# Softmax row sums of an attention block: ones-matmuls on TensorE, or accumulating DMAs through DRAM

## The chip, the cores and the metric

The kernel runs on one core of a Trainium2 chip. The metric is the device time of one execution in microseconds (us); lower is better. The engines are TensorE (PE, and PEld for its weight loads), VectorE (DVE), ScalarE (ACT), GpSimd (POOL) and SyncE (SP, which here only issues DMAs).

## The reference

Two kinds of blocks alternate twice, each adding to a residual `x` of 2048 rows by 1024 columns in float32:

```python
def _A_ref(x, wqkv, wo):                      # multi-head attention, H = 32 heads of Dh = 32
    qkv = (x @ wqkv).reshape(B, S, 3, H, Dh).transpose(2, 0, 3, 1, 4)
    q, k, v = qkv[0], qkv[1], qkv[2]
    p = softmax(einsum("bhqd,bhkd->bhqk", q, k) * Dh ** -0.5, axis=-1)
    o = einsum("bhqk,bhkd->bhqd", p, v)
    return o.transpose(0, 2, 1, 3).reshape(B, S, D) @ wo

def _B_ref(x, w_r, w_i):                      # spectral filter
    return irfft2(rfft2(x, axes=(-2, -1)) * (w_r + 1j * w_i), s=(S, D), axes=(-2, -1))

for _ in range(2):
    x = x + _A_ref(layernorm(x), wqkv, wo)
    x = x + _B_ref(layernorm(x), w_r, w_i)
```

## The kernel before, in words

`build` calls `attention` and `spectral` in turn, for layer 0 and layer 1.

**Attention.** The 32 heads form eight head groups (`g`, 0 to 7) of four heads, so that a group fills the 128 partitions. For each group the 2048 query rows are cut into four chunks (`c`) of 512, and the 2048 keys into 16 units (`kt`, counted from 0) of 128; `u` counts the 64 units of a group. One unit is:

- `S` (L726, L730): 12 score matmuls in float16 (three products of high and low halves for four heads) into two PSUM tiles `s` of 128x1024, from a pool of three; ScalarE turns each into a tile `p` of exponentials, keys on partitions, queries of two heads along the free dimension. The pool `at_p` has eight such tiles.
- `PV` (L736): four matmuls (two instructions each) that add P·V into the PSUM tile `o`; done for two units together at even `kt`. At the last unit of a chunk ScalarE copies `o` to the tile `oc` (one buffer).
- `add` (L747, L749): VectorE adds the two `p` tiles of 128x1024 to the accumulators `acc[0]`, `acc[1]`, one pair for all chunks.

The denominator of the softmax is the sum of `acc` over its 128 partitions. `fin` computes it at `kt == 0` of the next chunk, right behind the last `PV` of the old one: four matmuls with a matrix of ones (L756) into a PSUM tile of the scores' pool, then on VectorE a transpose by 32x32 blocks (L757), the reciprocal (L759), a running maximum for a check of the data (L760), a second transpose that spreads the reciprocals (L762) and the product with `oc` (L763). At `kt == 5`, `out` makes the high and low float16 halves (L769 on ScalarE, L770 on VectorE) and SP stores them to `od` in DRAM (L772).

On odd units TensorE gets a piece of other work: in groups 0 to 6 the projections of Q, K and V for the next groups (`filler`, L420, L477) with the splitting of their weights (`prep`, L215, L216); at the end of group 6 and in group 7 the output projection (`wo_parts`, L538), whose operands `load_o` reads back from `od`. The bound that the exponentials subtract is made a group ahead by `norms` and `mkbias`, the latter on POOL (L460 to L465).

The orders of TensorE and ScalarE in the main loop are the order of the program (`tc.manual_schedule`); VectorE's, POOL's and SP's are chosen by a planner, except that `tc.issue_after(x)` puts what is issued in its block behind instruction `x` on that engine. Each engine runs its queue in order.

**Looks at weights.** The kernel keeps the largest magnitude of its weights for a check. `look` reduces one piece of 128x1024 on VectorE (L328). In layer 0 the pieces are the high halves of the attention weights that lie in SBUF; in layer 1 they are 17 pieces of the spectral weights and 8 of `wo`, loaded for this into `lookp` by SP. One look is done at each `fin`, behind the last `add`.

**Spectral.** Its middle part runs over 32 units of frequencies. `loadw` loads the unit's weight tile `w` (two buffers), corrects some columns on VectorE (L1017) and changes signs on POOL (L1020); `fc` multiplies on VectorE and POOL (L1075 to L1084); TensorE does the transforms.

Of the kernel before, what the change touches and what calls it, by code (L numbers as in the profile page):

```python
# [6 lines left out]
F32 = mybir.dt.float32  # L7
# [229 lines left out]
class AttnPools:  # L237


    def __init__(self, tc):  # L240
        self.tc = tc
        self.low = Pools(tc, "left")
        self.big = self.low("at_x", 1).tile([128, 16384], F32, name="big")
        self.right = Pools(tc, "right")
        r = self.right("at_r", 1).tile([128, 16384], F32, name="R")
        self.x = r.rearrange("p (t d) -> p t d", d=1024)
        k = r.bitcast(F16).rearrange("p (t a n) -> p t a n", a=2, n=2048)
        self.k = [k[:, i] for i in (3, 4, 5)]
# [11 lines left out]
    def open_small(self):  # L260
        small = self.small = Pools(self.tc, "left")
        self.pp = small("at_p", 8)
        self.lookp = small("at_look", 2)
        self.qp = small("at_q", 1)
        self.oc = small("at_oc", 1)
        self.sgp = small("at_stage", 3)
        self.wqp = small("at_wqk", 2)
        self.wvp = small("at_wv", 1)
        self.sq = small("at_sq", 1)
        self.on = small("at_on", 2)  # L270
        self.on2 = small("at_on2", 2)
        self.sm = small("at_sm", 2)
        self.stages = [(self.sgp, "wst")] * 3 + [(self.on, "zt")] * 2 + [(self.on2, "ohl")] * 2


class Weights:
# [6 lines left out]
    def prep(self, ph, mid=None):  # L283
# [27 lines left out]
            yield  # L311
        if self.flag is not None:
            v = w[:, 0].rearrange("p d n -> p (d n)")
            self.unseen += [(v[:, o:o + 1024], None) for o in range(0, 512 * len(sl), 1024)]

    def take(self, i):

        if len(self.unseen) > i and self.unseen[i][1] is not None:
            src = self.unseen[i][1]
            t = self.ap.lookp.tile([128, 1024], F32, name="look")[:, :src.shape[1]]  # L320
            self.nc.sync.dma_start(t, src)
            self.unseen[i] = (t, None)

    def look(self):

        if self.unseen:
            self.take(0)
            self.nc.vector.tensor_reduce(self.cols.pop(0), self.unseen.pop(0)[0], axis=AX.X, op=ALU.max,  # L328
                                         apply_absolute_value=True)
            self.take(0)  # L330


SPILL = [2, 3, 8, 9]
# [3 lines left out]
def attention(nc, tc, layer, ap, xin, yd, wts, wo, cst, dram, flags):  # L337
# [171 lines left out]
    def load_wo():  # L509
# [89 lines left out]
    def wo_rest(t):  # L599
        p = psS.tile([128, 2, 512], F32, name="s")  # L600
# [115 lines left out]


    P, O, acc = {}, {}, ap.acc

    def S(g, c, kt):  # L720

# [20 lines left out]

    def add(g, c, kt):
        for hf in range(2):
            p = P[g, c, kt, hf]
            if kt == 1:
                nc.vector.scalar_tensor_tensor(acc[hf], P[g, c, 0, hf], 1e-34, p, op0=ALU.add, op1=ALU.add)  # L747
            elif kt:
                last_add = nc.vector.tensor_add(acc[hf], acc[hf], p)  # L749
        return last_add if kt > 1 else None  # L750

    def fin(g, c):
        zt = on.tile([128, 16, 32], F32, name="zt")
        z = psS.tile([128, 2, 512], F32, name="s")[:, 0]
        for h in range(4):
            nc.tensor.matmul(z[32 * h:32 * h + 32], cst["ones"], acc[h // 2][:, h % 2], start=True, stop=True)  # L756
        nc.vector.transpose(zt.rearrange("p a b -> p (a b)"), z)  # L757
        rc = sm.tile([128, 16], F32, name="rc")
        nc.vector.reciprocal(rc, zt[:, :, 0])  # L759
        nc.vector.tensor_max(flags["r"], flags["r"], rc)  # L760
        r = on.tile([128, 512], F32, name="zt")
        nc.vector.transpose(r.rearrange("p (a b) -> p a b", b=32), rc.unsqueeze(2).broadcast_to([128, 16, 32]))  # L762
        nc.vector.scalar_tensor_tensor(r, O[g, c], SO, r, op0=ALU.mult, op1=ALU.mult)  # L763
        O[g, c] = r

# [31 lines left out]
    with tc.manual_schedule(engines={mybir.EngineType.PE, mybir.EngineType.Activation}):  # L797
        for g in range(NG):
# [3 lines left out]
            for u in range(NCH * NKT):  # L802
# [4 lines left out]
                if kt % 2 == 0:  # L807
# [4 lines left out]
                    if kt == 0 and late:  # L812
                        for w in late:
                            last_add = add(*w)
                        with tc.issue_after(last_add.ins):
                            wts.look()
                        done = [late[1][:2]]
                        fin(*done[0])
                        late = []
                for w in late[:1]:  # L820
                    add(*w)
                late = late[1:]
                if kt == 5 and done:
                    out(*done.pop())
                pend.append((g, c, kt))
                if kt % 2 == 0:
# [3 lines left out]
                elif g == NG - 2:  # L830
# [103 lines left out]
def spectral(nc, tc, ap, yd, xout, a, cst, fast, flags=None, nxt=None, join=None):  # L934
# [70 lines left out]
    def loadw(i):  # L1005
# [301 lines left out]
def combine_flags(nc, ps, pool, flags, cst):  # L1307

    f = pool.tile([128, 6], F32, name="f4")
    fw, fb, fo = (pool.tile([128, 1], F32, name=n) for n in ("fwm", "fwbm", "fwom"))  # L1310
    for m, n in ((fw, "w"), (fb, "wb"), (fo, "wo")):
        nc.vector.reduce_max(m, flags[n], axis=AX.X)
    nc.vector.scalar_tensor_tensor(fw, fw, 1.0 / SW, fo, op0=ALU.mult, op1=ALU.max)
# [26 lines left out]
def build(nc, tc, a):  # L1340
    with ExitStack() as ctx:
# [9 lines left out]
        for h in range(4):  # L1351
# [2 lines left out]
        nc.vector.memset(cst["mhalf"], -0.5)  # L1354
        flags = {
            "mv": cp.tile([128, 32, 2], F32, name="fmv"),
            "w": cp.tile([128, 24], F32, name="fw"),
            "wb": cp.tile([128, -(-WOFF[-1] // 1024)], F32, name="fwb"),
            "wo": cp.tile([128, 8], F32, name="fwo"),
            "r": cp.tile([128, 16], F32, name="fr"),  # L1360
            "st": cp.tile([128, NST, 2, 6], F32, name="fst"),
            "bad": cp.tile([1, 1], I32, name="fi"),
# [8 lines left out]
        cols = [[f[:, i:i + 1] for i in range(f.shape[1])] for f in (flags["w"], flags["wb"], flags["wo"])]  # L1371
        later = [a["w"][:, o:min(o + 1024, WOFF[-1])] for o in range(0, WOFF[-1], 1024)]
        later += [a["wo"][128 * d:128 * d + 128, :] for d in range(8)]
        wts = [Weights(nc, ap, a["wp"], True, cols[0], []),
               Weights(nc, ap, a["wp"], None, cols[1] + cols[2], [(None, v) for v in later])]
# [48 lines left out]
```

## Time and profile before

| | |
|---|---|
| median of three runs (lowest, highest) | 3745.84 us (3744.72, 3746.28) |
| profiled execution, from its first to its last instruction | 3743.8 us |
| busy of that span: PE, PEld | 3683.9 us, 1644.2 us |
| busy of that span: DVE, ACT, POOL | 3194.1 us, 2931.6 us, 305.4 us |
| DMA issued by SP | 192.62 MB in 148992 packets |

The profile is of one execution. Its own time is given by its span; what lies around the span is not in it, and the median of the runs is 2.0 us above it. "Busy" is the time in which an engine had an instruction in work; the ends of matmuls are modelled, so a matmul's row can reach a little into the next one. A row of a group reads: line, engine, operation, output tile <- input tiles, shapes, count | busy us, mean ns of one | idle time of the engine just before them, and what ended it. A row of a timeline begins with its start and its length in us. DMA rows have the size of one and the median us from issue to landing.

### The profile page before, as it was taken

What the parts mean: (1) busy time and instruction counts of PE and PEld (TensorE: products, weight loads), DVE (VectorE), ACT (ScalarE), POOL (GpSimd) and SP (SyncE); (2) the same over time, 40 slices, a digit from 0 to 9 for tenths busy, and PEclk for the clock granted to TensorE, in tenths of its full rate; (3) what the DMA queues carried; (4) which work ended last, traced back from release to release, by engine and by line L of the source; (5) the groups of instructions that cost most, each with busy time, mean ns of one, the idle gap of its engine ahead of it and who ended that gap; (6) DMA issues with size and microseconds to landing.
All of it is one profiled execution on the core that took longest, in us unless ns stands there. A gap on an engine that the chain in (4) does not pass through costs nothing.

```text
span 3743.8 us, 80542 instructions
## 1 busy us (share of the span) xinstructions
PE 3683.9 (98%) x33367; PEld 1644.2 (44%) x33367; DVE 3194.1 (85%) x3842; ACT 2931.6 (78%) x3653; POOL 305.4 (8%) x406
## 2 busy tenths in 40 slices
PE   8999999999999999999999999999999999999998
PEld 5333433343343333378963334333433433333888
DVE  7799899989999978875658998999899999788754
ACT  5788888888888967758748888888888888677686
POOL 1000000000000000014410000000000000000243
PEclk9999999999999999999999999999999999999999
DMA  6000000000000211233250000101000102111423
GB/s 195 10 18 18 13 12 18 27 7 18 13 27 15 89 53 67 74 145 106 68 160 20 30 30 24 32 24 35 14 30 25 39 21 85 54 72 68 169 87 107
DMA packets 150697, 198.45 MB, mean 53 GB/s; under 512 B 58288, under 2 KB 105136, under 8 KB 149296
## 3 DMA queue, kind: packets, MB, share of 16 engines
q1 hardware_dynamic: 148992, 192.62, 15.8%
q8 instruction: 263, 4.31, 0.5%
q14 instruction: 114, 0.93, 0.1%
q10 hardware_dynamic: 1328, 0.59, 0.1%
HBM read 132.35 MB, written 48.23 MB: 48 GB/s over the span
## 4 chain that ended last, share of the span: by engine, by line


## 5 line engine op out<-in xcount | busy, mean ns | idle before, releaser
L730 ACT ACTIVATE p<-s,bias 128x1024 f32<-128x1024 f32 x2048 | 2169.7, 1111 | 515.9 <-PE s L726 497.7
L749 DVE TENSOR_TENSOR R<-R,p 128x1024 f32<-128x1024 f32 x1792 | 2090.1, 1218 | 137.3 <-ACT p L730 134.1
L736 PE MATMUL o<-p,R 128*32 128x512 f32 x8192 | 985.0, 598 | 0.0
L420 PE MATMUL x<-big,wqk 128*128 128x512 f16 x2880 | 676.4, 380 | 5.2 <-DVE Q L216 1.9
L726 PEld LDWEIGHTS <-R 32*128 32x128 f16 x12288 | 228.4, 92 | 738.7 <-issue 622.6
L420 PEld LDWEIGHTS <-wqk 128*128 128x128 f16 x3072 | 275.9, 98 | 422.1 <-issue 132.4
L736 PEld LDWEIGHTS o<-p,R 128*32 128x32 f32 x8192 | 213.7, 109 | 523.4 <-issue 523.4
L726 PE MATMUL s<-R 32*128 32x512 f16 x6144 | 425.5, 378 | 0.2
L726 PE MATMUL s<-Q,R 32*128 32x512 f16 x6144 | 425.4, 377 | 0.0
L477 PE MATMUL x<-wv,big 128*128 128x256 f16 x2784 | 330.7, 275 | 6.3 <-DVE R L216 4.6
L477 PEld LDWEIGHTS <-big 128*128 128x128 f16 x3072 | 291.7, 98 | 96.9 <-issue 56.1
L538 PE MATMUL x<-big 128*128 128x512 f16 x1008 | 231.9, 380 | 0.0
L460 POOL PARTITION_ALL_REDUCE mall<-mqk x16 | 38.4, 2400 | 2279.9 <-DVE mqk L454 2268.4
L538 PEld LDWEIGHTS <-big 128*128 128x128 f16 x1428 | 134.4, 98 | 164.6 <-issue 29.2
L747 DVE SCALAR_TENSOR_TENSOR R<-p 128x1024 f32<-128x1024 f32 x128 | 150.9, 1218 | 31.5 <-ACT p L730 31.5
L1084 DVE TENSOR_TENSOR H<-G,H 128x512 f16<-128x512 f32 (+1 forms) x68 | 46.6, 685 | 118.8 <-ACT H L1083 118.5
L1029 ACT COPY U<-ps 64x256 f32<-64x256 f32 (+1 forms) x272 | 97.0, 357 | 9.6 <-PE ps L1036 4.5
L757 DVE STREAM_TRANSPOSE zt<-s 128x512 f32<-128x512 f32 x64 | 45.8, 716 | 65.7 <-PE s L756 65.6
L1036 PE MATMUL ps<-cbi,H 128*128 128x256 f16 (+1 forms) x792 | 98.6, 273 | 3.3 <-ACT H L1083 2.3
L1029 ACT COPY B<-ps 64x256 f32<-64x256 f32 (+1 forms) x272 | 97.1, 357 | 5.6 <-PE ps L1036 2.1
L1036 PE MATMUL ps<-cb,big 128*128 128x256 f16 x780 | 96.7, 273 | 0.0
L1036 PEld LDWEIGHTS <-H 128*128 128x128 f16 (+1 forms) x792 | 76.5, 98 | 14.6 <-ACT H L1083 2.9
(449 smaller groups left out, 3012.1 us busy)
## 6 DMA issues: line engine op xcount, KB each, us to landing
wst<-in_wp SPq DMA_DIRECT2D x96, 256.0 KB, 3.0
R<-y SPq DMA_DIRECT2D x32, 512.0 KB, 5.5
w<-in_w SPq DMA_DIRECT2D x60, 256.0 KB, 2.7
od<-ohl SPq DMA_DIRECT2D x56, 256.0 KB, 2.4
big<-od SPq DMA_DIRECT2D x16, 896.0 KB, 5.3
y<-R SPq DMA_DIRECT2D x20, 512.0 KB, 2.6
wst<-in_wo SPq DMA_DIRECT2D x32, 256.0 KB, 2.6
xres<-in_x SPq DMA_DIRECT2D x16, 512.0 KB, 3.5
```

The source lines that it names most:

```text
L420: nc.tensor.matmul(ps, a, b, start=i == 0, stop=i == 23)
L477: nc.tensor.matmul(ps[:, j], x[c][:, d, o:o + 128], w[:, n, d], start=i == 0, stop=i == 23)
L538: nc.tensor.matmul(p, a, b, start=start and d == ds[0] and i == 0, stop=stop and d == ds[-1] and i == 2)
L726: nc.tensor.matmul(s[h // 2][:, h % 2], K[g][r, a, kt * 128:kt * 128 + 128], Q[g][r, b, c * 512:c * 512 + 512], start=i == 0, stop=i == 2)
L730: nc.scalar.activation(p, s[hf], AF.Exp, bias=bias[g], scale=SCALE / (SQ * SQ))
L736: nc.tensor.matmul(O[g, c][32 * h:32 * h + 32], V[g][:, kt, 32 * h:32 * h + 32], P[g, c, kt, h // 2][:, h % 2], start=kt == 0, stop=kt == ...
L747: nc.vector.scalar_tensor_tensor(acc[hf], P[g, c, 0, hf], 1e-34, p, op0=ALU.add, op1=ALU.add)
L749: last_add = nc.vector.tensor_add(acc[hf], acc[hf], p)
L757: nc.vector.transpose(zt.rearrange("p a b -> p (a b)"), z)
L1029: nc.scalar.copy(ov[64 * r:64 * r + 64, a0:a0 + m, x], tl[64 * x:64 * x + 64, :m, r])
L1036: nc.tensor.matmul(out, l, r, start=k == 0, stop=k == len(mm_) - 1)
L1084: nc.vector.tensor_sub(lo, gs, hi)
```

## The change

For head groups 0 to 6 the sum over partitions leaves TensorE. `partials` has POOL issue five DMAs: rows 0 to 31 of the accumulator are stored to a DRAM tile `zd`, rows 32 to 63, 64 to 95 and 96 to 127 are added to it by accumulating stores, and the result, now 32 partial sums for each query, is loaded into the SBUF tile `part`. In the next chunk, at `kt` 11, 12 and 13, `fold_partials` transposes `part` on VectorE, adds the 32 partial sums with a reduction of 128x512, and goes on as `fin` did; `out` follows at `kt` 14. The accumulators become two pairs that alternate by chunk. Group 7 keeps `fin` and its place.

The looks move: in layer 0 to `kt` 3 of chunks 1 to 3, and in group 7 to every second odd unit, and the eight pieces of `wo` are now looked at there in SBUF; layer 1 has none. The spectral weights are looked at in `loadw` of the first spectral stage. `load_o(1)` is issued behind the first projected tile instead of beside `load_o(0)`.

```diff
-        self.acc = [a[:, i] for i in (14, 15)]
+        self.acc = [a[:, 14:16]]
...
-        self.lookp = small("at_look", 2)
+        self.acc[1:] = [small("at_acc", 1).tile([128, 2, 2, 512], F32, name="acc")]
+        self.part = small("at_part", 1)
...
+            if layer == 0 and i % 2:
+                wts.unseen.append(wo_t[0][d // 4][:, d % 4])
...
         load_o(0)
-        load_o(1)
...
-            if t in (1, 7):
-                load_o(t // 4 + 2)
+            if t in (2, 1, 7):
+                load_o({2: 1, 1: 2, 7: 3}[t])
...
+    zd = [dram.tile([4, 32, 512], F32, name=f"zd{layer}{i}") for i in range(2)]
...
-            p = P[g, c, kt, hf]
+            p, a = P[g, c, kt, hf], acc[c % 2][:, hf]
...
+    def partials(g, c):
+        a, z = acc[c % 2], zd[c % 2]
+        for j in range(4):
+            nc.gpsimd.dma_start(z.rearrange("h p q -> p h q"), a[32 * j:32 * j + 32].rearrange("p a j n -> p (a j) n"),
+                                **({"accum_op": ALU.add} if j else {}))
+        part = O[g, c, 0] = ap.part.tile([128, 512], F32, name="part")
+        nc.gpsimd.dma_start(part, z.rearrange("h p q -> (h p) q"))
+
+    def fold_partials(g, c, after):
+
+        with tc.issue_after(after.ins):
+            fold_rows(g, c)
+        after = yield
+        with tc.issue_after(after.ins):
+            r = invert(O.pop((g, c, 1)))
+        after = yield
+        with tc.issue_after(after.ins):
+            times(g, c, r)
+        yield
+
+    def fold_rows(g, c):
+        zt = on.tile([128, 16, 32], F32, name="zt")
+        nc.vector.transpose(zt.rearrange("p a b -> p (a b)"), O.pop((g, c, 0)))
+        z = sm.tile([128, 16], F32, name="z")
+        nc.vector.tensor_reduce(z, zt, axis=AX.X, op=ALU.add)
+        O[g, c, 1] = z
...
-                        with tc.issue_after(last_add.ins):
-                            wts.look()
                         done = [late[1][:2]]
-                        fin(*done[0])
+                        (fin if done[0][0] == NG - 1 else partials)(*done[0])
                         late = []
                 for w in late[:1]:
-                    add(*w)
+                    last_add = add(*w)
                 late = late[1:]
-                if kt == 5 and done:
+                if kt == 3 and u > 3:
+                    with tc.issue_after(last_add.ins):
+                        wts.look()
+                if done and done[0][0] < NG - 1:
+                    if kt == 11:
+                        turn = fold_partials(*done[0], last_add)
+                    if 11 <= kt <= 13:
+                        turn.send(last_add if kt > 11 else None)
+                if done and kt == (5 if done[0][0] == NG - 1 else 14):
                     out(*done.pop())
...
                 elif g == NG - 1:
+                    if u % 4 == 1:
+                        wts.look()
...
         nc.sync.dma_start(wt, a["w"][:, WOFF[i]:WOFF[i + 1]])
+        if flags is not None:
+            nc.vector.tensor_reduce(flags["wb"][:, i:i + 1], wt, axis=AX.X, op=ALU.max, apply_absolute_value=True)
```

`fin` is cut into `normalize`, `invert` and `times`, which hold its instructions from L759 on in their order; `invert` ends with the spreading transpose, `times` is the product with `oc`.

More of the change, by code (lines that the diff above doesn't have):

```diff
@@ L313, in prep @@
             v = w[:, 0].rearrange("p d n -> p (d n)")
[L314 to L322, printed above, removed]
+            self.unseen += [v[:, o:o + 1024] for o in range(0, 512 * len(sl), 1024)]
     def look(self):
         if self.unseen:
-            self.take(0)
-            self.nc.vector.tensor_reduce(self.cols.pop(0), self.unseen.pop(0)[0], axis=AX.X, op=ALU.max,
+            self.nc.vector.tensor_reduce(self.cols.pop(0), self.unseen.pop(0), axis=AX.X, op=ALU.max,
                                          apply_absolute_value=True)
-            self.take(0)
 SPILL = [2, 3, 8, 9]
@@ L755, in fin, with normalize, invert @@
         for h in range(4):
-            nc.tensor.matmul(z[32 * h:32 * h + 32], cst["ones"], acc[h // 2][:, h % 2], start=True, stop=True)
+            nc.tensor.matmul(z[32 * h:32 * h + 32], cst["ones"], acc[c % 2][:, h // 2, h % 2], start=True, stop=True)
         nc.vector.transpose(zt.rearrange("p a b -> p (a b)"), z)
+        normalize(g, c, zt[:, :, 0])
+    def normalize(g, c, z):
+        times(g, c, invert(z))
+    def invert(z):
         rc = sm.tile([128, 16], F32, name="rc")
-        nc.vector.reciprocal(rc, zt[:, :, 0])
+        nc.vector.reciprocal(rc, z)
         nc.vector.tensor_max(flags["r"], flags["r"], rc)
@@ L762, in fin, with times @@
         nc.vector.transpose(r.rearrange("p (a b) -> p a b", b=32), rc.unsqueeze(2).broadcast_to([128, 16, 32]))
+        return r
+    def times(g, c, r):
         nc.vector.scalar_tensor_tensor(r, O[g, c], SO, r, op0=ALU.mult, op1=ALU.mult)
@@ L1309, in combine_flags @@
     f = pool.tile([128, 6], F32, name="f4")
[L1310 to L1311 removed]
+    fw, fb = (pool.tile([128, 1], F32, name=n) for n in ("fwm", "fwbm"))
+    for m, n in ((fw, "w"), (fb, "wb")):
         nc.vector.reduce_max(m, flags[n], axis=AX.X)
[L1313 removed]
+    nc.vector.tensor_scalar(fw, fw, 1.0 / SW, None, op0=ALU.mult)
     v = pool.tile([128, 1], F32, name="fv")
@@ L1356, in build @@
             "mv": cp.tile([128, 32, 2], F32, name="fmv"),
-            "w": cp.tile([128, 24], F32, name="fw"),
-            "wb": cp.tile([128, -(-WOFF[-1] // 1024)], F32, name="fwb"),
-            "wo": cp.tile([128, 8], F32, name="fwo"),
+            "w": cp.tile([128, 32], F32, name="fw"),
+            "wb": cp.tile([128, len(UNITS)], F32, name="fwb"),
             "r": cp.tile([128, 16], F32, name="fr"),
@@ L1370, in build @@
             nc.sync.dma_start(ap.x[:, 0, o:o + 512], x[0:128, o:o + 512])
[L1371 to L1375, printed above, removed]
+        wts = [Weights(nc, ap, a["wp"], True, [flags["w"][:, i:i + 1] for i in range(32)], []),
+               Weights(nc, ap, a["wp"], None, [], [])]
         for layer in range(2):
```

6 lines of the change are left out of this document (3 added, 3 removed).

## The prediction

> **What bounds the kernel now.** I read the page from the top: engine totals, then the 40 slices.
>
> ```profile
> PE 3683.9 (98%) x33367; PEld 1644.2 (44%) x33367; DVE 3194.1 (85%) x3842; ACT 2931.6 (78%) x3653; POOL 305.4 (8%) x406
> ...
> PE   8999999999999999999999999999999999999998
> ```
>
> TensorE is full nearly everywhere; over the whole span VectorE is the next busiest. "Busy" may hide waits, so the next view is the table of stretches: seven head groups of layer 0 and of layer 1, one tight chunk, head group 6 of layer 0, and the middle of the first spectral stage.
>
> ```profile
> core 0: us, PE busy (x) PEld busy (x) DVE busy (x) ACT busy (x) POOL busy (x), PEclk, DMA share, GB/s
> 149.10:1354.80 1205.70, 1202.94 (x11435) 424.61 (x11428) 1126.17 (x1162) 1009.37 (x1082) 28.34 (x28) 1.00 0.07 22
> 2012.80:3218.80 1206.00, 1202.82 (x11432) 424.69 (x11428) 1132.61 (x1174) 1009.39 (x1081) 28.82 (x28) 1.00 0.10 32
> 907.30:952.70 45.40, 45.40 (x412) 14.03 (x408) 43.29 (x46) 37.37 (x41) 1.23 (x1) 1.00 0.06 18
> 1177.70:1354.80 177.10, 175.50 (x1603) 53.62 (x1596) 168.93 (x176) 154.66 (x170) 3.98 (x4) 1.00 0.17 56
> 1668.00:1812.00 144.00, 139.07 (x1234) 127.23 (x1232) 70.96 (x184) 123.71 (x324) 68.87 (x100) 1.00 0.36 115
> ```
>
> A chunk (16 units) lasts 1205.70 / 27 = 44.66 us; VectorE works 1126.17 / 27 = 41.71 of them in layer 0 and 41.95 in layer 1, ScalarE 37.4. The granted clock is 1.00 in every row. So TensorE sets the pace, with VectorE some 3 us per chunk behind. TensorE's timeline around one chunk's end shows what the change takes out:
>
> ```profile
> 410.14 1.92 PE L736 MATMUL o<-p,R 128*32 128x512 f32 x16
> 412.00 0.82 PE L726 MATMUL s<-Q,R 32*128 32x512 f16 x12
> ...
> 415.37 1.92 PE L736 MATMUL o<-p,R 128*32 128x512 f32 x16
> 417.11 1.04 PE L756 MATMUL s<-R,ones 128*32 128x512 f32 x8
> 418.08 0.82 PE L726 MATMUL s<-Q,R 32*128 32x512 f16 x12
> ```
>
> An ordinary pair of P·V products is followed by the next scores 412.00 - 410.14 = 1.86 us later. At the chunk's end the ones-matmuls (L756) stand between: 418.08 - 415.37 = 2.71. They cost 0.85 us of TensorE, not the 1.04 of their row, and TensorE has no gap into which they could fall. At the first boundary of most head groups they cost more:
>
> ```profile
> 861.01 1.92 PE L736 MATMUL o<-p,R 128*32 128x512 f32 x16
> 862.75 1.20 PE L756 MATMUL s<-R,ones 128*32 128x512 f32 x8
> 863.88 0.82 PE L726 MATMUL s<-R 32*128 32x512 f16 x12
> ```
>
> Here it is 863.88 - 861.01 = 2.87, so 1.01 us; I count this at six boundaries of each layer.
>
> **The change part by part.**
>
> *Ones-matmuls of head groups 0 to 6, 28 per layer:* 44 x 0.85 + 12 x 1.01 = 49.5 us off TensorE, which is the path. Nothing else needs TensorE's place there: the scores' PSUM buffers come free a unit earlier, as at any other pair. Bounds: the whole L756 group (next fence), 68.9 / 64 x 56 = 60.3, and 0 where VectorE becomes late instead. I take 49.5.
>
> *VectorE's work per chunk.*
>
> ```profile
> L756 PE MATMUL s<-R,ones 128*32 128x512 f32 x512 | 68.9, 594 | 0.0
> L757 DVE STREAM_TRANSPOSE zt<-s 128x512 f32<-128x512 f32 x64 | 45.8, 716 | 65.7 <-PE s L756 65.6
> L762 DVE STREAM_TRANSPOSE zt<-rc 128x512 f32<-128x512 f32 x64 | 45.0, 704 | 0.0
> L328 DVE TENSOR_REDUCE fwb<-look 128x1 f32<-128x1024 f32 (+1 forms) x17 | 19.8, 1164 | 0.0
> L454 DVE TENSOR_REDUCE mqk<-s 128x1 f32<-128x512 f32 x32 | 21.8, 683 | 7.8 <-PE s L452 7.8
> L749 DVE TENSOR_TENSOR R<-R,p 128x1024 f32<-128x1024 f32 x28 | 32.6, 1217 | 1.2 <-ACT p L730 1.2
> ```
>
> The last row is of the tight chunk alone, the others of the whole span. The transpose from PSUM becomes one from SBUF (716 to 704 ns by L762). A reduction of 128x512 is new: 0.68 us by L454. Reciprocal, maximum, second transpose and scaling stay, at units 12 to 14 instead of in one block; the 65.6 us in which VectorE waited for L756 go. The adds are two of 128x1024 per unit before and after: 0. In layer 1 the 25 looks at weights (1.21 us each) and their loads go from VectorE and SP. In the tight chunk of layer 0 that leaves 43.29 + 0.68 = 43.97 us of VectorE against 45.40 - 0.85 = 44.55 of TensorE: 0.58 us to spare. In layer 1, 1.21 us more. The exponentials' buffers (eight, four units) let VectorE lag inside a chunk. But the tight chunk's adds wait 1.2 us for exponentials; if all of that stays, it falls 0.6 us short, and there are nine such chunks (the later three of head groups 0, 2 and 4): 5.6 us. Head group 6 of layer 0 is worse: 168.93 + 4 x 0.68 + up to two more looks, 2.4, is 174.1 against 177.10 - 3.4 = 173.7. I book 2 us for VectorE's tightness; bounds 0 and 25 (layer 0 gains nothing). The output conversion moves from unit 6 to unit 15, same work: 0; behind its store on SP stand weight loads that are issued a phase ahead, and the second load of outputs is put behind the first projected tile, with three tiles before its use. The copy of O is held until unit 14 instead of 2, and its buffer is next written at the chunk's end, two units later: 0. Eight looks at wo fall into layer 0's last groups, where group 7's VectorE has room.
>
> *The chain of five DMAs.* POOL issues a store of 32 partitions, three accumulating stores, each waiting for the one before, then a load; each 256 KB. No DMA of this trace accumulates or is issued by POOL. The nearest rows:
>
> ```profile
> wst<-in_wp SPq DMA_DIRECT2D x96, 256.0 KB, 3.0
> od<-ohl SPq DMA_DIRECT2D x56, 256.0 KB, 2.4
> L749 DVE TENSOR_TENSOR R<-R,p x1792: 1172/1218/1227, 111.8 to 3437.5; 128x1024 f32<-128x1024 f32 x200
> L460 POOL PARTITION_ALL_REDUCE mall<-mqk x16: 371/1230/4637, 96.5 to 3171.9; - x16
> L460 POOL PARTITION_ALL_REDUCE mall<-mqk x16 | 38.4, 2400 | 2279.9 <-DVE mqk L454 2268.4 <-issue 11.5
> 414.01 2.36 DVE L749 TENSOR_TENSOR R<-R,p 128x1024 f32<-128x1024 f32 x2 [0.25 <-ACT p L730]
> ...
> 442.74 2.36 DVE L749 TENSOR_TENSOR R<-R,p 128x1024 f32<-128x1024 f32 x2 [0.25 <-ACT p L730]
> ```
>
> Lower end 4 x 2.4 + 3.0 = 12.6 us. Upper end: an accumulating store reads and writes its target, 2.4 + 3.0 = 5.4, so 2.4 + 3 x 5.4 + 3.0 = 21.6, and five issues on POOL at the mean of its custom operation, 2.4 us, make 33.6. I take 2.4 + 3 x 4.0 + 3.0 + 5 x 1.2 = 23.4, nearer the stores and POOL's median. The time allowed: the chunk's last two adds end at 414.01 + 2.36 = 416.37, and the fold stands in VectorE's queue behind the add of the tenth unit, which ends at 445.10: 28.7 us. So the chain is covered and costs 0, with 5 us in hand. If the cover goes, everything behind the fold on VectorE waits (adds, low halves of Q, K and weights), then the exponentials' buffers, then ScalarE and TensorE. [...]
>
> *POOL's queue.* The score bound of the next head group is made there too:
>
> ```profile
> 1307.86 1.23 POOL L460 PARTITION_ALL_REDUCE mall<-mqk  x1 [222.56 <-DVE mqk L454]
> ...
> 1318.85 0.69 POOL L465 TENSOR_SCALAR bias<-bpr 128x1 f32<-128x1 f32 x1
> ```
>
> It holds POOL 11.7 us. Where it straddles a boundary (this one ends about 9 us past it) the chain has some 20 us left and may come 4 us late: at two such places I book 1 us in all. The bound itself, behind a chain, is needed a group later: 0.
>
> *First spectral stage.* Each of 32 weight tiles gets a VectorE reduction right behind its load, ahead of POOL's sign product.
>
> ```profile
> 1678.80 0.23 DVE L1017 SCALAR_TENSOR_TENSOR w<-w,wm 128x2 f32<-128x2 f32 x2 [2.24 <-DMA w<-in_w]
> ...
> 1681.22 0.39 PE L1036 MATMUL ps<-cbi,H 128*128 128x256 f16 x2 [1.67 <-ACT H L1083]
> L1017 DVE SCALAR_TENSOR_TENSOR w<-w,wm 128x2 f32<-128x2 f32 x18 | 3.3, 223 | 7.7 <-DMA w<-in_w 7.7
> ```
>
> 32 x 0.68 = 22 us of work fit into VectorE's 144 - 71 idle us. But nine tiles already make VectorE wait 7.7 us for their loads, and one such wait reached TensorE (1.67 us). At 32 tiles of this kind the waits would be 27 us, 20 more; the share that reached TensorE, 1.67 / 7.7, makes 4 us of them, which I take; bounds 0 and 20.
>
> **Sum.** 3743.8 (span) - 49.5 + 2 + 1 + 4 = 3701.3; the median of the runs stands 2.0 above the span, so 3703 us.
>
> **The rivals.**
>
> *The chain is late (slower).* The place is the fold at unit 12. At the upper end, 33.6 us, VectorE would wait 4.9 us a chunk: layer 0's chunk 41.71 + 0.68 + 4.9 = 47.3 against 44.66, layer 1's 41.95 - 1.21 + 0.68 + 4.9 = 46.3, so 28 x 2.6 + 28 x 1.7 = 120 us, about 3866. It turns the sign where the wait passes the spare 2.3 us (layer 0) to 3.2 us (layer 1), a chain of 31.5 us or 6.3 per DMA. For it: L460 runs from 371 to 4637 ns for one operation, so POOL is held up at times, while the adds never pass 1227 ns. Against it: 256 KB stores land in 2.4 us. [...]
>
> *VectorE sets the pace in layer 0.* If its waits for exponentials cannot be squeezed below what they are, layer 0 keeps its time: half the gain, 3743.8 - 25 + 5 + 2 = 3726. For it: 0.58 us to spare in 44.55. Against: four units of buffers, and the bunch at the boundary is spread.
>
> *Nothing changes.* A chain of 30 to 32 us gives all back: within 7.5 us of 3746.
>
> **How the numbers follow.** Forecast 0.67 (own range 3690 to 3712: the three costs at 0 and the ones-matmuls halfway to their bound, or the costs at more than twice my values); VectorE in layer 0 0.15 (3712 to 3732); no change 0.05; late chain 0.13. A measurement can tell about 0.2% (7.5 us). Faster 0.82, same 0.05, slower 0.13. The range 3685 to 3732 takes in the first two and the L756 group's 60 us.
>
> **What would show it.** Right: no L756 before the last head group; 2.71 us from P·V to scores becomes 1.86; chunks of 44.66 become about 43.8; the reduction near 0.68 us without a wait for the part's load in front; last landing under 28 us after the last add. Wrong: VectorE idle at the fold's transpose with the load as releaser; gaps of ScalarE behind unit 12; chunks of layer 0 unchanged while layer 1's shrink; waits for w on VectorE above 10 us in the first spectral stage.

## The result, and the profile after

The changed kernel takes 3793.05 us (median of 4 runs, 3789.14 to 3795.87) against 3746.06 us before: a ratio of 1.0121, 95% interval 1.0107 to 1.0135. It is 47 us slower, where 3703 us was forecast. One of the ten executions of the run e10_probe below, 6186.73 us long at a granted clock of 0.62, belongs to a slow state and is not in that run's ratio. The profiled execution has a span of 3794.0 us. First its totals, from the page:

```profile
PE 3668.2 (97%) x32919; PEld 1638.2 (43%) x32919; DVE 3212.4 (85%) x3912; ACT 2942.4 (78%) x3653; POOL 552.0 (15%) x686
```

TensorE has 448 instructions less and is busy 15.7 us less, in a span 50 us longer: it waits. It is idle for 125.8 us, 59.9 before. It was also slower while it worked: the ones-matmuls taken out are worth some 44 us (worked out below), so the other matmuls were busy some 28 us longer, and the granted clock over the span is 0.989 instead of 0.997. Where it waits, the table of stretches of the changed kernel tells. Its first three rows are the seven head groups of layer 0 (before 1205.70), the first spectral stage with what stands around it, from the last copy of O in layer 0 to the first in layer 1, and the seven head groups of layer 1 (before 1206.00). The fourth is a few us of TensorE after a wait, and comes later.

```profile
core 0: us, PE busy (x) PEld busy (x) DVE busy (x) ACT busy (x) POOL busy (x), PEclk, DMA share, GB/s
149.80:1385.40 1235.60, 1194.86 (x11220) 420.90 (x11216) 1141.70 (x1195) 1012.66 (x1081) 136.79 (x164) 0.99 0.24 50
...
1605.00:2049.00 444.00, 423.54 (x3470) 324.96 (x3472) 301.84 (x595) 304.26 (x581) 120.95 (x165) 0.98 0.33 104
2049.00:3269.90 1220.90, 1189.93 (x11220) 420.40 (x11216) 1115.07 (x1169) 1012.43 (x1082) 159.89 (x164) 0.99 0.25 51
636.36:641.00 4.64, 4.64 (x20) 1.63 (x23) 4.64 (x6) 0.00 (x0) 0.00 (x0) 0.63 0.01 4
```

Layer 0 grew by 29.9 us, layer 1 by 14.9 and the spectral stage by 6.4 (437.6 before). TensorE stood idle for 41 us in layer 0 and 31 us in layer 1, where it had been idle for 3 in each. The list of waits of the changed kernel says for whom (us in total, times, longest):

```profile
PE x L411 <- DVE R L216: 29.2, 19, 4.7
PE s L719 <- DVE mqk L445: 17.4, 16, 2.4
PE x L531 <- DVE R L557: 12.9, 2, 8.1
PE x L411 <- DVE Q L216: 10.4, 9, 3.1
```

None of these is a wait for exponentials, the place where I had looked for a late VectorE. They are the projections, which wait until L216 has emptied their one PSUM bank `x`; the scores, which wait until L445 has read the norms out of a tile of their pool; and the output projection, whose 12.9 us come with late chains (0.9 in the run e2_defer, where no chain is late). All are small VectorE instructions that stand in the queue behind additions and the fold. Here is one such place, at units 12 to 14 of a chunk of head group 3: VectorE, then TensorE.

```profile
714.20 4.64 DVE L742 TENSOR_TENSOR acc<-acc,p 128x1024 f32<-128x1024 f32 x4
718.74 0.72 DVE L767 STREAM_TRANSPOSE zt<-part 128x512 f32<-128x512 f32 x1
719.49 0.69 DVE L769 TENSOR_REDUCE z<-zt 128x16 f32<-128x512 f32 x1
720.10 2.35 DVE L742 TENSOR_TENSOR acc<-acc,p 128x1024 f32<-128x1024 f32 x2
722.36 0.25 DVE L785 RECIPROCAL rc<-z 128x16 f32<-128x16 f32 x1
...
722.74 0.70 DVE L788 STREAM_TRANSPOSE zt<-rc 128x512 f32<-128x512 f32 x1
723.36 0.65 DVE L445 TENSOR_REDUCE mqk<-s 128x1 f32<-128x512 f32 x1
```

```profile
721.41 0.39 PE L719 MATMUL s<-Q,R 32*128 32x512 f16 x2
724.07 0.82 PE L719 MATMUL s<-Q,R 32*128 32x512 f16 x10 [2.27 <-DVE mqk L445]
724.82 3.03 PE L729 MATMUL o<-p,R 128*32 128x512 f32 x16
```

VectorE goes from one instruction to the next without idle time. The normalisation (L767 to L788) stands in front of the reduction L445, and TensorE stops for 2.27 us.

At the same time a hole has opened elsewhere. The next rows are VectorE at the end of the tight chunk, first in the kernel before, then in the changed one:

```profile
905.49 1.21 DVE L328 TENSOR_REDUCE fw<-wqk 128x1 f32<-128x1024 f16 x1
908.00 0.72 DVE L757 STREAM_TRANSPOSE zt<-s 128x512 f32<-128x512 f32 x1 [1.30 <-PE s L756]
...
909.94 0.69 DVE L763 SCALAR_TENSOR_TENSOR zt<-oc,zt 128x512 f32<-128x512 f32 x1
910.54 2.35 DVE L747 SCALAR_TENSOR_TENSOR R<-p 128x1024 f32<-128x1024 f32 x2
```

```profile
913.56 2.36 DVE L742 TENSOR_TENSOR acc<-acc,p 128x1024 f32<-128x1024 f32 x2
917.80 2.36 DVE L740 SCALAR_TENSOR_TENSOR R<-p 128x1024 f32<-128x1024 f32 x2 [1.88 <-ACT p L723]
920.07 1.22 DVE L320 TENSOR_REDUCE fw<-wqk 128x1 f32<-128x1024 f16 x1
```

The first addition of a chunk takes two units together, so at a chunk's end VectorE has for some us nothing to add. Before, the look and the whole normalisation lay there (905.49 to 910.54). Now nothing does: VectorE waits 1.88 us, and has the work to do at units 12 to 14, where the rows above show it without a gap.

The second new loss is the late chain. The group of the fold's transpose on the page of groups:

```profile
L767 DVE STREAM_TRANSPOSE zt<-part 128x512 f32<-128x512 f32 x56 | 39.8, 710 | 22.1 <-DMA part<-zd 22.1
```

These 22.1 us are six waits out of 56. One of them, from its cause to its end: POOL; then VectorE; then TensorE.

```profile
590.17 7.51 POOL L451 PARTITION_ALL_REDUCE mall<-mqk  x1 [18.86 <-DVE mqk L445]
604.39 1.13 POOL L453 TENSOR_TENSOR bpr<-mall 128x1 f32<-128x1 f32 x1 [6.71 <-issue]
605.60 1.46 POOL L454 TENSOR_TENSOR bpr<-bpr,half 128x1 f32<-128x1 f32 x1
607.15 0.68 POOL L456 TENSOR_SCALAR bias<-bpr 128x1 f32<-128x1 f32 x1
607.90 0.76 POOL L748 DMA_DIRECT2D zd<-R  x1
...
625.70 0.61 POOL L751 DMA_DIRECT2D part<-zd  x1 [4.97 <-DMA zd<-R]
```

```profile
589.94 4.63 DVE L742 TENSOR_TENSOR R<-R,p 128x1024 f32<-128x1024 f32 x4
594.48 0.69 DVE L799 TENSOR_TENSOR ohl<-zt,ohl 128x512 f16<-128x512 f32 x1
595.08 2.36 DVE L742 TENSOR_TENSOR R<-R,p 128x1024 f32<-128x1024 f32 x2
...
628.76 0.71 DVE L767 STREAM_TRANSPOSE zt<-part 128x512 f32<-128x512 f32 x1 [3.41 <-DMA part<-zd]
```

```profile
636.36 4.44 PE L411 MATMUL x<-big,wqk 128*128 128x512 f16 x12 [4.67 <-DVE R L216]
```

The chunk's last additions end at 595.08 + 2.36 = 597.44, but POOL is held by the score bound until 607.83 and issues the chain's first DMA at 607.90, 10.5 us late. From there to the fold it takes 20.9 us. VectorE loses 3.41 us at unit 12, and TensorE then 4.67.

### The profile page after: what moved, and what is told of

Its sections match the earlier page's. It is cut to its first block, busy times and chain, and to the rows that moved or that the text cites. A ratio compares the mean times of both kernels' runs of the same rounds, so it can differ in the third digit from the quotient of the medians.

```text
span 3794.0 us, 79849 instructions
## 1 busy us (share of the span) xinstructions
PE 3668.2 (97%) x32919; PEld 1638.2 (43%) x32919; DVE 3212.4 (85%) x3912; ACT 2942.4 (78%) x3653; POOL 552.0 (15%) x686
## 4 chain that ended last, share of the span: by engine, by line
## 5 line engine op out<-in xcount | busy, mean ns | idle before, releaser
L742 DVE TENSOR_TENSOR R<-R,p 128x1024 f32<-128x1024 f32 x896 | 1047.5, 1221 | 59.0 <-ACT p L723 56.9
L742 DVE TENSOR_TENSOR acc<-acc,p 128x1024 f32<-128x1024 f32 x896 | 1046.6, 1221 | 52.1 <-ACT p L723 50.5
L411 PE MATMUL x<-big,wqk 128*128 128x512 f16 x2880 | 686.8, 384 | 41.1 <-DVE R L216 29.2
L719 PE MATMUL s<-Q,R 32*128 32x512 f16 x6144 | 427.1, 379 | 11.3 <-DVE mqk L445 11.3
L531 PE MATMUL x<-big 128*128 128x512 f16 x1008 | 236.5, 385 | 13.0 <-DVE R L557 12.9
L748 POOL DMA_DIRECT2D zd<-R x112 | 92.7, 827 | 857.6 <-DVE R L742 583.0
L748 POOL DMA_DIRECT2D zd<-acc x112 | 91.7, 819 | 863.7 <-DVE acc L742 572.5
L740 DVE SCALAR_TENSOR_TENSOR R<-p 128x1024 f32<-128x1024 f32 x64 | 75.5, 1222 | 104.6 <-ACT p L723 104.6
L740 DVE SCALAR_TENSOR_TENSOR acc<-p 128x1024 f32<-128x1024 f32 x64 | 75.9, 1223 | 38.0 <-ACT p L723 38.0
```

The source lines that it names most:

```text
L411: nc.tensor.matmul(ps, a, b, start=i == 0, stop=i == 23)
L531: nc.tensor.matmul(p, a, b, start=start and d == ds[0] and i == 0, stop=stop and d == ds[-1] and i == 2)
L719: nc.tensor.matmul(s[h // 2][:, h % 2], K[g][r, a, kt * 128:kt * 128 + 128], Q[g][r, b, c * 512:c * 512 + 512], start=i == 0, stop=i == 2)
L740: last_add = nc.vector.scalar_tensor_tensor(a, P[g, c, 0, hf], 1e-34, p, op0=ALU.add, op1=ALU.add)
L742: last_add = nc.vector.tensor_add(a, a, p)
L748: nc.gpsimd.dma_start(z.rearrange("h p q -> p h q"), a[32 * j:32 * j + 32].rearrange("p a j n -> p (a j) n"), **({"accum_op": ALU.add} if ...
```

## The experiments

Three theories were told apart: the normalisation's new place on VectorE costs the time (by normalisation the text means all from the fold's transpose to the product with `oc`); the late chains do; the DMA traffic itself does, through memory or queues. A fourth was that only the added reduction of 0.69 us counts. The medians of before that the ratios use lie between 3745.80 and 3746.61 us.

**e1_next: the fold one chunk later, in the hole.**

```diff
+                        if waiting:
+                            done = [waiting.pop()]
+                            with tc.issue_after(last_add.ins):
+                                fold_rows(*done[0])
+                                times(*done[0], invert(O.pop((*done[0], 1))))
...
-        self.oc = small("at_oc", 1)
+        self.oc = small("at_oc", 2)
-    ... dynamic_dma_scratch_size=4096)
+    ... dynamic_dma_scratch_size=2048)
```

> The fold of a chunk's partial sums moves from units 12 to 14 of the next chunk to the end of that chunk, behind its last add, so one chunk later; the DMAs and all else stay as in the changed kernel (oc gets a second buffer). Theory A, place on VectorE: the changed kernel loses because normalisation left the chunk's end, where VectorE waits for the second unit's exponentials anyway (1.88 us idle there now), and stands in the middle of the chunk, where VectorE has none to spare. By it chunks without extra looks fall to their time before minus 0.85, about 3715 us in all (3746 - 49.5 + 6 for the spectral stage + 12 for the looks heaped into head group 6). Theory B, only late chains: POOL is held by the score bound and six folds wait 22 us; then about 35 us come back, 3758. Theory C, the 280 DMAs or POOL slow the other engines: no better than 3785.

Measured: 3722.53 us, ratio 0.9931 (0.9914 to 0.9948). With the same DMAs and the same work on VectorE, only elsewhere in its queue, the change becomes a gain, though 7.5 us above the 3715 of theory A. With the fold the output conversion moves back to `kt` 5, `oc` gets a second buffer, and the scratch memory of POOL's DMAs is halved. None of these was tried by itself; in the changed kernel's trace no instruction waits for `oc`. The row of the projections in the groups of this kernel shows 12.3 us of waits where the changed kernel had 41.1:

```profile
L411 PE MATMUL x<-big,wqk 128*128 128x512 f16 x2880 | 677.2, 381 | 12.3 <-DVE Q L216 7.1 <-DVE R L216 2.6 <-ACT R L472 1.9
```

This version cures both the place and the late chains, since a chain now has a whole chunk more; the next two take them apart.

**e2_defer: the score bound behind the next chain on POOL, instead of ahead of it.**

```diff
-            mkbias(g)
+            if g:
+                held.append(g)
+            else:
+                mkbias(g)
...
+        while held:
+            with tc.issue_after(last.ins):
+                mkbias(held.pop(0))
```

> The score bound of the next head group is made on POOL behind the next chain of five DMAs instead of ahead of it; all else as in the changed kernel. Theory B: the six folds that wait for their load no longer do, the chunks with them lose their excess over like chunks (5.2, 8, 2.5, 6.6, 5.2 and 7.6 us), 3793 - 35 = 3758. Theory A agrees on these 35 but expects the other chunks unchanged (45.86 in the chunk that is 45.42 before). Theory C: no change.

Measured: 3762.98 us, ratio 1.0043 (1.0026 to 1.0060), 30.1 us less than the changed kernel. No fold waits any more; its row in the groups of this kernel:

```profile
L773 DVE STREAM_TRANSPOSE zt<-part 128x512 f32<-128x512 f32 x56 | 39.3, 703 | 0.0
```

So six late chains, 22.1 us of VectorE's waits, cost the kernel 30 us: TensorE is idle 20.7 us less than in the changed kernel and busy 12.5 us less.

**e3_nodma: no chain of DMAs; the fold at its place reads a constant tile.**

```diff
+    fixed = ap.part.tile([128, 512], F32, name="part")
+    nc.vector.memset(fixed, 64.0)
...
-        nc.gpsimd.dma_start(part, z.rearrange("h p q -> (h p) q"))
+        O[g, c, 0] = fixed
```

> No chain of DMAs at all: the fold at units 12 to 14 reads a tile of constants (left out: the row sums of head groups 0 to 6, and the wait for them); VectorE's instructions keep kind, number and place. Theory A: only the six waits and what they cost go, 3758 as in the deferred bound, and 45.86 stays in the chunk that was 45.42. Theory C, transfers or POOL slow something: about 3705 to 3715.

Measured: 3759.86 us, ratio 1.0037 (1.0023 to 1.0051). That is e2 within the runs' spread, and layer 1 agrees to 0.1 us (1201.1 and 1201.0 us for 27 chunks). The 280 DMAs, 73.4 MB, cost no more than the runs' spread of some us as long as they are in time. The theory of the traffic falls.

**e4_ones: ones-matmuls in all groups at their old place, the rest of the change kept.**

```diff
-                        (fin if done[0][0] == NG - 1 else partials)(*done[0])
+                        fin(*done[0])
...
-                if done and kt == (5 if done[0][0] == NG - 1 else 14):
+                if done and kt == 5:
```

> All eight head groups take the ones-matmuls and the place of before; the rest of the change stays (moved looks, looks at w in the first spectral stage, two accumulator pairs). What these cost by themselves: 6.4 us in the spectral stage by the two traces, and in layer 0 the looks, eight of them heaped into two chunks of head group 6, up to 10 us; 3752 to 3762. If the looks are innocent, 3752.

Measured: 3767.37 us, ratio 1.0057 (1.0040 to 1.0074), 5 us above the range expected. Layer 1, which has lost its looks, needs 1205.1 us (before 1206.1). Layer 0 needs 15 more; the table of stretches for it:

```profile
148.90:1369.70 1220.80, 1206.96 (x11432) 425.49 (x11428) 1131.55 (x1168) 1009.39 (x1081) 30.02 (x28) 1.00 0.07 22
```

The looks are what differs between the layers here, so their new places cost about 15 us by themselves: half of it in two chunks of head group 6 (49.07 and 49.10 us instead of 45.01 and 45.81), the rest in the chunks with a look at unit 3 beside projections, 0.7 to 1.1 us each.

**e8_place: the kernel before, with only reciprocal, maximum, second transpose and scaling moved to units 12 and 13 and `out` to 14** (and, for that, `load_o(1)` behind the first projected tile, as in the changed kernel).

```diff
+                if done and done[0][0] < NG - 1 and kt in (12, 13):
+                    with tc.issue_after(last_add.ins):
+                        if kt == 12:
+                            r12 = invert(O.pop((*done[0], 1)))
+                        else:
+                            times(*done[0], r12)
```

> The kernel before, ones-matmuls, looks and all, with one thing moved: VectorE's reciprocal, maximum, spreading transpose and product with oc (1.8 us) leave the chunk's end and stand at units 12 and 13 of the next chunk, the output conversion at 14 (the second load of outputs moves as in the changed kernel). No work is added and none removed. Theory A, place: the chunks with projections of Q and K, which TensorE fills now, get 0.3 to 1 us longer, 8 to 30 us in all, 3754 to 3776. Theory D, that only the added 0.68 us of reduction matters: no change, 3746.

Measured: 3771.77 us, ratio 1.0069 (1.0052 to 1.0085). No instruction is added on any engine and no DMA is on POOL; 1.8 us of VectorE's work a chunk stands some 30 us later, the output conversion (0.7 us) moves back with it, and the kernel is 26 us slower. So the place of the work costs time without any added work, and the theory that only the added reduction counts falls. But TensorE waits for something else here than in the changed kernel, namely for the chunk's last additions, which the ones-matmuls read:

```profile
L755 PE MATMUL s<-R,ones 128*32 128x512 f32 x512 | 81.4, 595 | 8.4 <-DVE R L748 8.4
```

Before, this group was busy for 68.9 us and waited for nothing, so 12.5 + 8.4 = 20.9 of the 26 us lie here, at matmuls that the changed kernel no longer has in these head groups. The waits for L216 in the projections and for the norms sum to 5.8 us, 8.0 before. This run therefore shows that the place matters, and not by how much in the changed kernel; that is e1 against e2.

**e5_pin: e1, and the looks of layer 0 kept out of head group 6 but for one.**

```diff
-                if kt == 3 and u > 3:
+                if kt == 3 and (u > 3 and g < NG - 2 or u == 35 and g == NG - 2 and layer == 0):
...
+                        with tc.issue_after(last_add.ins):
+                            wts.look()
```

> As the kernel with the fold one chunk later (3722), with the looks kept out of head group 6 but for one: the last piece of the attention weights at unit 3 of its third chunk, the eight of wo in group 7, each behind the add of its unit, where the planner cannot pull it forward. Theory: the nine looks (five and three in two chunks, one in a third) are what makes two chunks of head group 6 of layer 0 48.9 and 49.1 us long instead of about 44.3 and 45.2 as in layer 1; they give 8 us back, 3714. Rival: those chunks are long from the fold itself; then nothing moves.

Measured: 3714.13 us, ratio 0.9915 (0.9899 to 0.9932), the fastest version. In e1, as in the changed kernel, the planner had put five looks into the second chunk of head group 6, three into the third and one into the last; these chunks were 48.9, 49.1 and 43.0 us long and are now 44.3, 46.3 and 43.0. The seven head groups of the two layers in this kernel:

```profile
148.80:1339.50 1190.70, 1180.02 (x11220) 418.00 (x11215) 1139.13 (x1182) 1008.66 (x1080) 134.74 (x164) 1.00 0.25 52
2003.30:3187.10 1183.80, 1179.10 (x11220) 417.90 (x11216) 1120.84 (x1164) 1008.68 (x1080) 133.66 (x164) 1.00 0.25 52
```

**e6_best and e7_wlate_after: the reductions of 23 spectral weight tiles moved behind the tiles' last use**, in e5 and in the changed kernel.

```diff
...
+        elif flags is not None:
+            seen[i] = wt
...
+        if i in seen:
+            nc.vector.tensor_reduce(flags["wb"][:, i:i + 1], seen.pop(i), axis=AX.X, op=ALU.max, apply_absolute_value=True)
```

> As the previous kernel, and in the first spectral stage the reduction of 23 of the 32 weight tiles (those that VectorE does not correct) stands behind the tile's last use instead of behind its load. Theory: the stage's 6 to 8 us over before come from VectorE waiting for the loads and POOL waiting for VectorE (1.9 us of idle before single reductions); 4 to 6 of them come back, 3709. Rival: it is the 22 us of work itself, or the tile's buffer held 0.7 us longer; then no change or slower.

> The changed kernel with that one edit of the spectral stage alone: 3793 - 5 = 3788 if the theory of the waits holds, 3793 if not. Attention is untouched, so its chunks must keep their times.

Measured: e6 3715.65 us, 0.9917 (0.9901 to 0.9934), the same as e5; the stage stayed (444.7 against 443.7 us). So the wait for a weight tile's load in front of the reduction, my ground for the 4 us, isn't what lengthens the stage. e7 took 3774.29 us, 1.0074 (1.0058 to 1.0091): 18.8 us less than the changed kernel, but not in that stage (445.6 against 444.0). The chunks did not keep their times as expected, though TensorE, VectorE, ScalarE and POOL have the same order of instructions in head groups 0 to 6 as in the changed kernel's trace. Three folds waited there, 10.0 us in all, not six: POOL's reductions fell otherwise, which the next run bears on.

**e10_probe: the kernel before, with five small operations on POOL at the ninth unit of each chunk.**

```diff
+    def probe(p):
+        t = sm.tile([128, 2, 64], F32, name="pr")
+        i = nc.gpsimd.tensor_copy(t[:, 0], p[:, 0, 0:64])
+        with tc.issue_after(i.ins):
+            i = nc.gpsimd.memset(t[:, 1], 0.0)
+        ... (a second memset, a copy from t[:, 1] to t[:, 0], a third memset)
```

> The kernel before with five small POOL operations of 128x64 per chunk in head groups 0 to 6, at the ninth unit, in this order: a copy that reads an exponential tile, two memsets, a copy that reads what the memset wrote, a memset. Theory P (an operation of POOL that reads SBUF is held while VectorE runs additions of two SBUF inputs back to back; one that only writes is not): both copies end 0.23 to 0.24 us behind the end of a VectorE instruction, with lengths spread from about 0.2 to several us, and the memsets all have one length of a few tenths of a us whatever VectorE does. Rival Q (POOL's first operation after a long idle time is slow): only the first copy is stretched. Rival R (everything on POOL is held by VectorE's additions): memsets are stretched as well. By all three the time is that of the kernel before, 3746 within 5 us, since nothing waits for these results but the buffer of the tile read.

Measured: 3746.96 us, ratio 1.0001 (0.9991 to 1.0011). The view of one line each (min, median and max in ns), for the two copies and the first memset:

```profile
L778 POOL COPY pr<-p x56: 236/3258/7746, 123.3 to 3191.5; 128x64 f32<-128x64 f32 x56
```

```profile
L784 POOL COPY pr<-pr x56: 236/1143/15677, 123.9 to 3192.1; 128x64 f32<-128x64 f32 x56
```

```profile
L780 POOL MEMSET pr<- x56: 143/148/154, 123.5 to 3191.7; 128x64 f32 x56
```

Both copies are stretched, up to 66 times, the memsets never. The longest copy on POOL's timeline, and VectorE's under its end:

```profile
1244.30 15.68 POOL L784 COPY pr<-pr 128x64 f32<-128x64 f32 x1
```

```profile
1255.26 4.62 DVE L749 TENSOR_TENSOR R<-R,p 128x1024 f32<-128x1024 f32 x4
1259.80 0.68 DVE L216 SCALAR_TENSOR_TENSOR R<-x,R 128x512 f16<-128x512 f32 x1
```

It ends at 1259.98, 0.10 us behind the end of the additions at 1259.88 and 0.18 us into the L216 that follows, which takes one of its inputs from PSUM. The longest of the first copies, 7.74 us from 389.78, ends 0.09 us behind a run of VectorE instructions with two inputs in SBUF, whose last additions end at 397.43. So in this run POOL's copies, which read SBUF, were held while VectorE ran such instructions back to back, and took 0.24 to 15.68 us; the memsets, which only write, took 0.14 to 0.15. Expected offset: 0.23 to 0.24 us, measured 0.09 and 0.10 at these two places; the offset expected was that of the longer reduction. The score bound's reduction was held in the same way: in the POOL fence above it ends at 590.17 + 7.51 = 597.68, 0.24 us behind the run of additions that ends at 597.44. In the changed kernel's trace every one of the 14 reductions made during head groups ends 0.23 to 0.24 us behind the end of a VectorE instruction, the first, second or seventh after its start.

**e9_nolook: e5 without the reductions of the spectral weights.**

```diff
-            nc.vector.tensor_reduce(flags["wb"][:, i:i + 1], wt, axis=AX.X, op=ALU.max, apply_absolute_value=True)
+            nc.gpsimd.memset(flags["wb"][:, i:i + 1], 0.0)
```

> The version with the fold a chunk later and the looks kept out of head group 6 (3714.1 us), with the 32 reductions of the spectral weights left out (a POOL memset of one column each stands for them; the check of the data loses that part). Theory W (the reductions themselves, or what they delay on VectorE, lengthen the first spectral stage): the stage goes from 443.7 back to about 437.5 us, the kernel to about 3708. Rival X (they are hidden, and the stage is longer because other work of the changed kernel lies there differently): the stage stays at 443 to 445 us, the kernel at 3714.

Measured: 30887.03 us. The zeros made the kernel's check of its data choose its slow second path behind the fast one, so the total says nothing. The fast path comes first in the trace, and up to the spectral stage it has the stretches of e5 (149.2, 1190.7 and 220.1 us against 148.8, 1190.7 and 220.1). The stage itself, in e5 and then in this kernel:

```profile
1559.60:2003.30 443.70, 423.29 (x3469) 324.43 (x3471) 301.86 (x595) 303.19 (x580) 121.51 (x165) 0.98 0.32 104
```

```profile
1559.90:1997.90 438.00, 419.12 (x3470) 323.20 (x3471) 283.59 (x560) 301.72 (x580) 120.75 (x165) 0.99 0.33 105
```

Without the reductions it takes 438.0 us, as before the change. They cost the 6 us, though VectorE has some 140 us of idle time in this stage, and by e6 they cost it also with 23 of them behind the tile's last use. Through which buffer they reach TensorE was not tried.

## Why the prediction was wrong

The runs give the way from 3745.80 us to the changed kernel in four steps, each the difference of two medians:

| step | us |
|---|---|
| before to e5: the change with the fold in the hole and the looks kept apart | -31.7 |
| e5 to e1: the looks as the planner heaps them | +8.4 |
| e1 to e2: the normalisation at units 12 to 14, the output conversion at 15 | +40.5 |
| e2 to the changed kernel: the score bound ahead of the chain on POOL | +30.1 |

**Ones-matmuls, -49.5: right in kind, some 5 us too high.** In the chunks that have no Q and K projections beside them, where VectorE keeps up, a chunk falls from 45.28 to 44.42 us and from 46.20 to 45.34: 0.86, against 0.85 forecast. Layer 1 of e5 makes 1183.80 / 27 = 43.84 us a chunk; "about 43.8" was forecast. At the twelve boundaries priced at 1.01 a chunk falls by 0.59 only (44.13 to 43.54 and 44.72 to 44.14, e4 to e5 in layer 1). In sum a layer gains 1205.1 - 1183.8 = 21.3 us in 27 chunks and 0.86 in the next, so 44 us in two. The gain is real and was eaten elsewhere.

**VectorE's work per chunk, +2 (bounds 0 and 25): the step that failed.** The prices were right (the reduction 686 ns, 0.68 forecast). The assumption was not: "The exponentials' buffers (eight, four units) let VectorE lag inside a chunk." They cover a lag of the additions. They don't cover the evacuations in the same queue, which empty a single bank, nor the norms' reduction: TensorE's waits for L216 in the projections and for the norms sum to 60.1 us in the changed kernel, to 48.5 in e2, where no chain is late, to 20.9 in e1 and to 8.0 in the kernel before. From e1 to e2 they grow by 27.6 of the 40.5 us; TensorE's busy time, with the same instructions, grows by 12.9 more, at a granted clock over the span of 0.993 instead of 0.996. I compared VectorE's sum per chunk with TensorE's, 43.97 to 44.55, and took 0.58 us to spare for the question. In the tight chunk of the changed kernel VectorE is idle for 2.5 us of 45.86, but 1.88 of them lie in the hole at the boundary. What decided was at which unit the work stands. I had even written that "the bunch at the boundary is spread" as a point in favour; the boundary was the one place where it cost nothing. This term measured 40 us (e1 to e2), the output conversion's place, `oc`'s second buffer and the scratch size included.

**Looks, booked within the same term: mis-sized.** "Up to two more looks" in head group 6 of layer 0 were nine, five of them in one chunk: 8.4 us. The three chunks of head groups 1, 3 and 5 with a look at unit 3 beside projections grew by 2.8 us each; the same look costs them 1.1 us where the normalisation stands at the boundary (44.73 to 45.85 in e4). So the two pieces of work, each small, cost more together than apart.

**The chain, 0: right for the chain, 23.4 us forecast and 20.9 in the fence above.** By the page of the changed kernel its stores landed 3.9 and 4.1 us after their issue (medians, one plain store among each four) and its load 3.0, where the forecast's sum has 2.4, three times 4.0 and 3.0. That an accumulating store reads and writes its target, the ground of the upper end, has no row of its own. 50 of 56 chains were hidden.

**POOL's queue, +1: wrong by 29 us, the second step that failed.** Both parts of the mechanism stood in the prediction and were not put together. It said that the score bound holds POOL near a boundary and that L460 runs from 371 to 4637 ns. But it read the spread as something that befalls the chain, took 11.7 us as the hold (17.7 at 590.17), counted two places where there were six, and stopped at 4 us of VectorE's wait without asking what that does to TensorE. The chain's DMAs themselves were not held: their issue on POOL took 0.57 to 0.99 us. The size is in part luck, since it hangs on how the reductions fall: e7, with the same attention, stands only 11.3 us above e2.

**First spectral stage, +4 (0 to 20): 6.4, near by luck, with the wrong reason.** The waits for loads in front of the reductions were 6.7 us, not 27, and moving the reductions changed nothing (e6).

**The rivals.** None came as written. "VectorE sets the pace in layer 0" had the right engine, priced as the loss of the gain and no more, in one layer of two. "The chain is late" had the right place and sign, with a slow chain as its cause; the chain was quick and started late. I treated the two as cases that exclude each other, and they came together. Of the signs listed as wrong, VectorE did idle at the fold's transpose with the load as releaser; of the signs of being right, the chunks did not come down to 43.8 us but went up to 1235.60 / 27 = 45.76 and 1220.90 / 27 = 45.22.

## What to carry to other kernels

Before work is moved along an in-order queue, look for the holes of that engine unit by unit. An average with 6% to spare says nothing about the unit in which the work will stand, and work that lies in a hole is free only there. For an engine that lags, list every buffer that it empties and every result that others read from it: in the changed kernel the shallowest, one PSUM bank, set the lag that TensorE could stand (42.7 us of waits for L216), not the deep pool of the main stream (no wait for exponentials). When something with a deadline is given to an idle engine, ask what else stands ahead of it in that queue and what can stretch that.

## What the runs showed of the hardware

**After two stalls TensorE was slow for some us.** The window row 636.36 to 641.00 at the top shows a granted clock of 0.63 behind the wait of 4.67 us: 12 projection matmuls took 4.44 us. Elsewhere in this trace the same 12 take 2.76, as here:

```profile
944.30 2.76 PE L411 MATMUL x<-big,wqk 128*128 128x512 f16 x12
```

So this stall cost 1.7 us more than itself; from 637.50 to 639.00 the granted clock is 0.50. Behind the wait of 2.27 us at 724.07 the 16 P·V matmuls took 3.03 us instead of 1.92, at a granted clock of 0.61. That goes some way to explain how 22.1 us of late folds became 30 us; it was not taken apart.

**The same POOL reduction was 1.23 or 7.51 us long.** The one at 590.17 in the changed kernel starts 0.23 us into a run of additions and is held for the whole run; in e7 its counterpart starts 0.23 us into the same run and is through after the first addition. In the changed kernel the chain starts 10.5 us behind the chunk's last additions, in e7 2.4 (598.32 against 595.97), with no edit near; part of e7's 18.8 us is that. In these two traces the reductions start 0.21 to 0.23 us into a run, and the starts do not sort the lengths. What decides whether the reduction gets in is open.
